# Attention and a two-layer MLP on one core: the last two token tiles as one 2×2 block problem

## The chip, the cores and the metric

The kernel runs on one core of one Trainium2 chip. The metric is the device time of one execution in microseconds (us), as the median of the runs shown. The core has a matmul engine (PE, with its weight loads listed apart as PEld), three elementwise engines (DVE, ACT and POOL) and a queue, SP, from which this kernel issues all its DMAs. Each engine works through its own queue in order; the engines wait for each other through semaphores.

## What is computed

Attention with a causal mask over 4 batches, 12 heads, 448 positions and 64 values per head, then a two-layer MLP over all 1792 tokens (768 to 2048 to 768):

```python
scores = scale * np.matmul(q, k.transpose(0, 1, 3, 2))
scores = np.where(mask, -1000000000.0, scores)
attn = np.exp(scores - np.max(scores, axis=-1, keepdims=True))
attn = attn / (np.sum(attn, axis=-1, keepdims=True) + 1e-09)
x = concat_heads(np.matmul(attn, v))            # 1792 x 768
h = x @ w_in                                    # 768 x 2048
g = np.where(h > 0.0, h, np.exp(np.minimum(h, 0.0)) - 1.0)
out = g @ w_out                                 # 2048 x 768
```

q, k and v are 32-bit floats, the two weight matrices 64-bit floats, which the kernel first turns into 32-bit ones on the chip.

## The kernel before

**Tiles.** The 448 positions are cut into four chunks of 112. A token tile is one chunk of all four batches: 4 x 112 = 448 columns. The text counts tiles from 1 to 4; the code's `g` counts from 0. Everything is kept transposed: features lie on the 128 partitions, tokens on the 448 columns. So layer 1 of a tile is 16 (`FT`) by 6 (`KT`) block products of 128x128 weights with 128x448 values, layer 2 is 6 (`ET`) by 16.

**A block product.** `three` (L580 to L585) computes one with three matmuls, to keep 32-bit precision: value and weight are each split into a rounded part and a rest (`xh`/`xl`, `gh`/`gl`; `whl` holds both parts of a weight piece), and high x high, high x low and low x high are summed in PSUM. The first 8 rows of layer 1 of tile 1 (`PLAIN`) use one plain 32-bit matmul instead (L599). A split costs one rounding copy (ACT, or DVE) and one subtraction (DVE, or POOL): L571, L572 and L574 for weight pieces, L316 and L318 for the attention's output, L611 and L612 for layer 1's.

**Order of the MLP.** `layers` (L633) goes through layer 1 row by row (`emit_h`, the ELU at L606 to L612 closes a row), then layer 2 (`emit_o`; L629 copies a finished row out of PSUM, L631 sends it). `weights` (L530) makes a weight piece: for tile 1 it loads 64-bit numbers, converts them (L547 to L558) and stores them as 32-bit in DRAM (L561); for tiles 2 to 4 it loads them back (L564). A piece is one row of layer 1 (768 columns) or, in layer 2, 768, 768 and 512 columns (`FG`).

**Attention.** `attention(g)` yields lumps of work: scores (L424, or L430 for tile 2), softmax (L269 on DVE, L273 on ACT), division by the sums (L500 to L506), transposes (L475), copies out of PSUM (L479, L480) and the product with the values (L454). Attention of tile 1 runs first, by itself. The loop at L646 to L660 then mixes each later tile's attention into the layers of the tile before it, in proportion: tile 2's beside tile 1's layers, tile 3's beside tile 2's, tile 4's beside tile 3's. Tile 4's layers have nothing beside them.

**Who orders the work.** Every operation is handed to `Plan.add` with its possible engines, a cost and a due time; `Plan.run` (L103) then lists the operations by due time against these costs and so fixes each engine's queue, and for operations with several `ways` also the engine. Buffers come from rings (`BUFS`, L226): five `w` tiles for raw weight pieces and eight `w6` tiles for split pieces are used in turn, so a load into `w` waits for all readers of the piece five places earlier.

## Time and profile before

| | us |
|---|---|
| median of 3 runs (lowest, highest) | 664.85 (663.88, 665.50) |
| profiled execution, its span from first to last instruction | 662.8 |
| busy: PE, PEld, DVE, ACT, POOL | 647.7, 550.8, 435.9, 414.5, 124.3 |
| granted TensorE clock, mean | 0.996 |
| DMA: bytes, share of 16 engines | 114.8 MB, 56.3% |

The profiled execution's own time is its span; the runs' times hold in addition what lies before the first and after the last instruction, 664.85 - 662.8 = 2.05 us at the median. Times in rows are us from the span's start, durations us or, where marked, ns. The busy time of an engine is the union of its records; neighbouring records overlap a little, so counts times mean durations come to more than the busy time.

### The profile page before, as it was taken

To read this page: it belongs to the slowest core of one execution; us is meant where nothing else is said; L and a number is where in the kernel's file an instruction comes from. 1 tells how busy PE (TensorE), PEld (TensorE's weight loads), DVE (VectorE), ACT (ScalarE), POOL (GpSimd) and SP (SyncE) were. 2 spreads that over 40 slices of the span, in tenths; PEclk is the share of its full clock that TensorE was granted. 3 is DMA by queue.
4 is the path that set the end of the run, shared out by engine and by line. 5 is a ranking of instruction groups with operands and counts; after the bars stand their busy time and mean duration, and the time that the engine had idled before them with its cause. 6 is when DMAs were issued, how large, how long until landed. Compare 5 with 4: busy or idle time off the path is not lost.

```text
span 662.8 us, 11710 instructions
## 1 busy us (share of the span) xinstructions
PE 647.7 (98%) x4176; PEld 550.8 (83%) x4176; DVE 435.9 (66%) x1032; ACT 414.5 (63%) x940; POOL 124.3 (19%) x104
## 2 busy tenths in 40 slices
PE   5899999999999999999999999999999999999997
PEld 4655588888878888888888888888888999999996
DVE  5866689786858897776562778687576447764310
ACT  6997999977549767675442987777565424443200
POOL 1353344343333212111000231102000100000000
PEclk9899999999999999999999999999999999999999
DMA  9999677788957464365564346364435543233210
GB/s 219 289 366 374 204 236 252 234 289 271 327 171 232 125 186 117 103 180 168 163 190 144 105 131 195 104 179 134 122 106 160 166 146 113 86 112 103 68 29 28
DMA packets 83577, 114.79 MB, mean 173 GB/s; under 512 B 39104, under 2 KB 59072, under 8 KB 83520
## 3 DMA queue, kind: packets, MB, share of 16 engines
q1 hardware_dynamic: 83520, 114.06, 56.3%
q8 instruction: 33, 0.54, 0.3%
q14 instruction: 24, 0.20, 0.1%
HBM read 95.94 MB, written 18.09 MB: 172 GB/s over the span
## 4 chain that ended last, share of the span: by engine, by line
PE 83%; ACT 10%; DVE 4%; issue 1%; POOL 1%; DMA 1%; SPq 0%; POOLq 0%; ACTq 0%; DVEq 0%
PE op L583 10%; PE op L585 10%; PE op L584 10%; PE hp L583 9%; PE hp L585 9%; PE hp L584 9%; PE av L454 6%; PE tr L475 6%; PE hp L599 6%; PE sc L424 5%; ACT a L273 3%; ACT w L551 2%; DVE whl L574 1%; ACT whl L571 1%; PE sc L430 1%
## 5 line engine op out<-in xcount | busy, mean ns | idle before, releaser
L574 DVE TENSOR_TENSOR whl<-w,whl 128x768 fp32r<-128x768 f32 (+1 forms) x118 | 114.3, 971 | 48.2 <-ACT whl L571 46.1
L583 PE MATMUL op<-gh,whl 128*128 128x448 f32 x384 | 143.4, 374 | 0.0
L585 PE MATMUL op<-gh,whl 128*128 128x448 f32 x384 | 141.1, 367 | 0.9 <-DVE whl L574 0.6
L584 PE MATMUL op<-gl,whl 128*128 128x448 f32 x384 | 140.4, 366 | 0.0
L583 PE MATMUL hp<-xh,whl 128*128 128x448 f32 x336 | 126.5, 376 | 0.3 <-ACT whl L571 0.3
L585 PE MATMUL hp<-xh,whl 128*128 128x448 f32 x336 | 122.9, 366 | 0.5 <-DVE whl L574 0.5
L584 PE MATMUL hp<-xl,whl 128*128 128x448 f32 x336 | 122.8, 366 | 0.0
L273 ACT ACTIVATE a<-a,nm 112x112 f32<-112x112 f32 (+3 forms) x192 | 96.9, 518 | 26.3 <-DVE nm L269 26.3
L269 DVE CUSTOM_DVE_ANT_0 a<-sc,mask 112x112 f32<-112x112 f32 (+3 forms) x192 | 75.1, 443 | 31.0 <-PE sc L424 20.8
L571 ACT ACTIVATE whl<-w 128x768 fp32r<-128x768 f32 (+1 forms) x69 | 53.9, 789 | 53.8 <-PE op L585 42.1
L583 PEld LDWEIGHTS op<-gh,whl 128*128 128x128 f32 x384 | 72.1, 188 | 9.8 <-issue 2.8
L585 PEld LDWEIGHTS op<-gh,whl 128*128 128x128 f32 x384 | 72.1, 188 | 9.2 <-DVE whl L574 3.2
L558 POOL TENSOR_TENSOR w<-w,w 128x768 int32<-128x768 int32 (+1 forms) x34 | 61.4, 1807 | 93.3 <-DVE w L552 42.8
L584 PEld LDWEIGHTS op<-gl,whl 128*128 128x128 f32 x384 | 72.2, 188 | 5.7
L583 PEld LDWEIGHTS hp<-xh,whl 128*128 128x128 f32 x336 | 63.1, 188 | 10.3 <-issue 4.7
L585 PEld LDWEIGHTS hp<-xh,whl 128*128 128x128 f32 x336 | 63.1, 188 | 6.1 <-DVE whl L574 0.9
L584 PEld LDWEIGHTS hp<-xl,whl 128*128 128x128 f32 x336 | 63.2, 188 | 4.8 <-issue 0.2
L608 DVE SCALAR_TENSOR_TENSOR hp<-m,hp 128x448 f32<-128x448 f32 x64 | 40.0, 625 | 30.4 <-ACT m L607 30.2
L606 ACT ACTIVATE m<-hp 128x448 f32<-128x448 f32 x64 | 34.7, 542 | 36.3 <-PE hp L585 34.8
L611 ACT ACTIVATE gh<-hp 128x448 fp32r<-128x448 f32 x64 | 34.3, 537 | 28.1 <-DVE hp L608 28.1
L612 DVE TENSOR_TENSOR gl<-hp,gh 128x448 fp32r<-128x448 f32 x64 | 39.7, 621 | 18.5 <-ACT gh L611 18.1
L454 PEld LDWEIGHTS av<-at,v 112*64 112x64 f32 x864 | 41.6, 137 | 12.1 <-issue 9.5
(57 smaller groups left out, 843.6 us busy)
## 6 DMA issues: line engine op xcount, KB each, us to landing
w<-w_i SPq DMA_DIRECT2D x48, 384.0 KB, 3.5
w<-w_o SPq DMA_DIRECT2D x36, 384.0 KB, 3.1
w<-in_w_in SPq DMA_DIRECT2D x16, 768.0 KB, 7.3
w<-in_w_out SPq DMA_DIRECT2D x12, 768.0 KB, 6.3
k<-in_qk SPq DMA_DIRECT2D x30, 224.0 KB, 4.1
w_i<-w SPq DMA_DIRECT2D x16, 384.0 KB, 5.2
q<-in_qk SPq DMA_DIRECT2D x24, 224.0 KB, 4.5
out_t<-ob SPq DMA_DIRECT2D x24, 224.0 KB, 3.0
```

What stands on the lines that cost most here:

```text
L269: plan.add(dve(n, lambda: nc.vector.tensor_tensor_reduce(out=a()[:, c], in0=sc()[:, c], in1=mask[:, S - n:], op0=ALU.add, op1=ALU.min, sca ...
L273: plan.add(act(n, lambda: nc.scalar.activation(a()[:, c], a()[:, c], AF.Exp, bias=nm()[:, x:x + 1], scale=-1.0, accum_out=su()[:, x:x + 1] ...
L454: nc.tensor.matmul(av()[half_of(half), chunk(o["b"])], o["v"]()[:, half, i], at()[:, chunk(x)], start=i == 0, stop=i == g,)
L475: nc.tensor.transpose(tr()[:, chunk(x)], o["a"][half]()[:, chunk(i)], ident)
L558: plan.add(pool(size, lambda: nc.gpsimd.tensor_tensor(out=wf().bitcast(I32), in0=wf().bitcast(I32), in1=low().bitcast(I32), op=ALU.add)), ...
L571: act(size, lambda: nc.scalar.activation(wh()[:, :n], w()[:, :n], AF.Copy)),
L574: sub = lambda eng: lambda: eng.tensor_tensor(out=wl()[:, :n], in0=w()[:, :n], in1=f32(wh()[:, :n]), op=ALU.subtract)
L583: nc.tensor.matmul(acc(), wh()[:, k], xh(), start=first, stop=False)
L584: nc.tensor.matmul(acc(), wh()[:, k], xl(), start=False, stop=False)
L585: nc.tensor.matmul(acc(), wl()[:, k], xh(), start=False, stop=last)
L599: pe(ONE, lambda: nc.tensor.matmul(hp(), w[0]()[:, k], x(), start=k == 0, stop=k == KT - 1), [*w, x], [hp], due)
L608: plan.add(dve(S, lambda: nc.vector.scalar_tensor_tensor(out=hp(), in0=m(), scalar=-1.0, in1=hp(), op0=ALU.add, op1=ALU.max)), [m], [hp])
```

## The change

Tiles 3 and 4 are no longer computed one after the other. Their layers become one problem of 2x2 blocks: the weights are cut in halves of rows and of inputs, the values in halves of features and in the two tiles. It is computed with seven block products of half size instead of eight, numbered 1, 2, 6, 7, 4, 5, 3 (`GROUPS`): layer 1 in `mixed_h`, layer 2 in `mixed_o`. The pieces of the method:

- **Values.** `halves` forms sums and differences of value blocks, four subtractions for each set of four blocks, before product 6; each product then splits its own 128x448 blocks into high and low (`split_row`).
- **Weights.** While tile 2's layers run, `mixed` forms the weight combinations with four additions per pair of pieces (on DVE or POOL, in place in the `w` tiles) and stores them in DRAM (`sin`, `sout`). To have both pieces of a pair at hand, tile 2 takes its rows in the order 0, 8, 1, 9 and so on, and its layer 2 in two accumulators side by side. The products read back pieces of 768 columns (`raw_piece`), 56 in all.
- **Results.** Products are combined as they finish: `results` keeps product 1 (`take`) and adds 6 and 7 to it (`plus`); products 2 and 3 go on in the PSUM bank of 1 and 5.
- **Layer 2 pieces** are 512 columns for all tiles, two runs of two blocks, so 24 pieces for 18.
- **Attention** of tiles 2, 3 and 4 is spread over the layers of tiles 1 and 2 alone (`SPREAD`, in units of the plan's matmul cost; the two tiles' layers are 246 such units). Tiles 3 and 4 have no attention beside them.
- **Buffers.** Tiles of 128x448 share one pool of places (`ROWS`), PSUM banks another; after the attention its places go to the new products (`lend`, `Heap`).

```diff
...
-    FG = ((0, 6), (6, 6), (12, 4))
+    HALF_F, HALF_K, HALF_E = FT // 2, KT // 2, ET // 2
+    NX = HALF_F // 2
...
-        xl = new("xl", [P, S], F32R)
+        if g >= 2:
+            x = xs[g, p] = new("x", [P, S], name="xs")
+            plan.add([
+                act(S, lambda: nc.scalar.activation(x(), av(), AF.Copy)),
+                dve(S, lambda: nc.vector.tensor_copy(x(), av())),
+            ], [av], [x])
+            return
...
-            f0, n = FG[key[2]]
-            src = w_out[key[1], :, f0:f0 + n]
+            two = slice(2 * key[2], 2 * key[2] + 2)
+            src, home = (
+                x[key[1]].rearrange("p (h f) c -> p h f c", h=2)[:, :, two] for x in (w_out, kout)
+            )
+            n = 4
...
-            k = kept[key] = Buf(None, lambda: dram.tile([P, n, P], F32, name=name))
+            k = kept[key] = Buf(None, lambda: home)
...
+    def mixed(layer, r, x, wa, wb):
+
+
+        h = HALF_K if layer == 1 else 2
+        n = h * P
+        blk = lambda w, half: lambda: w()[:, half * h:half * h + h]
+        a, b = (lambda half: blk(wa, half)), (lambda half: blk(wb, half))
+        add(b(1), b(0), b(1), n, ALU.add, [(wb, 0)], [(wb, 1)])
+        add(b(0), a(0), b(0), n, ALU.subtract, [(wa, 0)], [(wb, 0)])
+        add(a(0), b(1), a(0), n, ALU.subtract, [(wb, 1)], [(wa, 0)])
+        add(a(1), a(1), a(0), n, ALU.subtract, [(wa, 0)], [(wa, 1)])
+        k = skept[layer, r, x] = Buf(None, lambda: None)
+        home = sin[r] if layer == 1 else sout[x, :, :, :, r]
+        for i, w in enumerate((wa, wb)):
+            dma(2 * h * 64, 2 * P, lambda i=i, w=w: nc.sync.dma_start(
+                out=home[:, :, i], in_=w()[:, :2 * h].rearrange("p (h k) c -> p h (k c)", h=2)
+            ), [w], [(k, i)])
...
+            if g == 1 and f >= HALF_F:
+                plan.cap = due + LATER
+                mixed(1, f - HALF_F, None, wt[g, "i", f - HALF_F][3], wt[g, "i", f][3])
+                plan.cap = 1e9
...
-        x = f // FG[0][1]
-        if f == FG[x][0]:
+        x, i = f % HALF_F // 2, f // HALF_F * 2 + f % 2
+        if i == 0:
             weights(g, ("o", e, x))
-        if f == 0:
-            st["o"] = new("hp", [P, S], name="op")
-        op = st["o"]
+        first, last = x == i == 0, x == NX - 1 and i == 3
+        if i == 0 and g == 1 and e >= HALF_E:
+            plan.cap = due + LATER
+            mixed(2, e - HALF_E, x, wt[g, "o", e - HALF_E, x][3], wt[g, "o", e, x][3])
+            plan.cap = 1e9
...
+        fs = range(FT) if g == 0 else [f + h for f in range(HALF_F) for h in (0, HALF_F)]
+        for f in fs:
...
+        by_x = [(x, 2 * x + i + h) for x in range(NX) for h in (0, HALF_F) for i in range(2)]
+        for e in range(ET if g == 0 else HALF_E):
+            if g == 0:
+                todo = [(e, f) for _, f in by_x]
+            else:
+                todo = [(d, f) for x in range(NX) for d in (e, e + HALF_E) for y, f in by_x if y == x]
+            for d, f in todo:
+                yield THREE, lambda due, d=d, f=f: emit_o(g, d, f, due)
...
+    def halves(bs, i):
+
+        if i == 1:
+            return bs[0, 0]
+        if i == 2:
+            return bs[1, 0]
+        if i == 6:
+            t1, t2 = bs[0, 0], row("t2")
+            minus(t1, bs[0, 1], t1)
+            minus(t2, bs[1, 1], t1)
+            minus(bs[0, 1], bs[1, 1], bs[0, 1])
+            minus(bs[1, 0], bs[1, 0], t2)
+            return t2
+        return {7: bs[0, 1], 4: bs[1, 0], 5: bs[0, 0], 3: bs[1, 1]}[i]
...
+    def raw_piece(srcs, reads, dst):
+        w, t = new("ws", [P, KT, P], name="w"), new("w6s", [P, 2, KT, P], F32R, "whl")
+        dma(KT * 64, 2 * P, lambda: nc.sync.dma_start(out=dst(w()), in_=srcs), reads, [w])
+        hi_lo(lambda: t()[:, 0], lambda: t()[:, 1], w, KT * P, (t, 0), (t, 1), w)
+        ring("ws").done(w)
+        return t, (lambda k: t()[:, 0, k]), (lambda k: t()[:, 1, k])
...
+    GROUPS = ((1, 2), (6, 7, 4), (5, 3))
+    MIX = {6: (0, 0), 7: (0, 1), 3: (1, 0), 5: (1, 1)}
...
+        if i == 1:
+            keep["s", r] = row("s1")
+            take(keep["s", r], acc)
+        elif i == 6 or i == 7:
+            keep[i, r] = row("u")
+            plus(keep[i, r], acc, keep["s", r] if i == 6 else keep[6, r])
...
+        def item(g, i, r, k, due):
+            if k == 0:
+                if i not in (2, 3):
+                    st[r] = new("bank", [P, S], name="hp")
+                st["w", i, r] = weights_of(i, r)
+            acc, w, x = st[r], st["w", i, r], parts[i, k]
+            first = k == 0 and i not in (2, 3)
+            last = k == HALF_K - 1
+            pe(THREE, lambda: three(acc, w, k, x, first, last, i in (2, 3)), [w[0], *x], [acc], due)
+            if not last:
+                return
+            results(i, r, acc, keep)
+            if i == 2:
...
+            elif i == 4:
+                plus(acc, acc, keep[7, r])
+                G[1, 0, r] = keep["s", r]
+                elu(G[1, 0, r], acc)
+            elif i == 5:
+                G[1, 1, r] = keep[7, r]
+                plus(G[1, 1, r], acc, G[1, 1, r])
+                elu(G[1, 1, r], G[1, 1, r])
+            elif i == 3:
+                plus(acc, acc, keep[6, r])
+                G[0, 1, r] = keep[6, r]
+                elu(G[0, 1, r], acc)
+            if i not in (1, 5):
+                banks.done(acc)
+            if i in (2, 3) or i == 4 and r % 2 or i == 7:
+                ring("w6s").done(w[0])
...
+        for g in range(3):
+            for j in range(HALF_F // 2):
+                for i in GROUPS[g]:
+                    for r in (2 * j, 2 * j + 1):
+                        for k in range(HALF_K):
...
+            if e == f == 0:
+                st["w"] = weights_of(i, x)
+                st["x"] = []
+                for y in (2 * x, 2 * x + 1):
+                    b = halves({(a, c): G[a, c, y] for a in range(2) for c in range(2)}, i)
+                    st["x"].append(split_row(b))
+                    if i not in (1, 2):
+                        rows.done(b)
...
+            first = x == f == 0 and i not in (2, 3)
+            last = x == NX - 1 and f == 1
+            pe(THREE, lambda: three(acc, w, e * 2 + f, g, first, last, i in (2, 3)), [w[0], *g], [acc], due)
...
+        for i in (i for g in GROUPS for i in g):
+            for x in range(NX):
+                for e in range(HALF_E):
+                    for f in range(2):
+                        yield THREE, lambda due, a=(i, x, e, f): item(*a, due)
...
+    SPREAD = (0.0, 125.0, 185.0, 240.0)
...
+    ls = [(c, fn, g == 0) for g in range(2) for c, fn in layers(g)]
+    at = []
+    for g in range(1, NG):
+        items = list(attention(g))
+        all_c, done_c = sum(c for c, _ in items), 0.0
+        for c, fn in items:
+            at.append((SPREAD[g - 1] + (SPREAD[g] - SPREAD[g - 1]) * done_c / all_c, c, fn))
+            done_c += c
+    moved = 0.0
...
+            while at and at[0][0] <= moved:
+                _, ca, fa = at.pop(0)
+                fa(t)
+                t += ca * (SLOW if early else 1.0)
+                if not at:
+                    after_attention()
...
+    run([(c, fn, False) for c, fn in mixed_h()])
+    run([(c, fn, False) for c, fn in mixed_o()])
...
```

How this moves instructions is shown at three places. Names with a number are single buffers; `whl` is a split weight piece, `w` a raw one, `tr` and `at` attention weights before and after their copy out of PSUM, `sc` scores, `rr` reciprocal sums.

DVE in layer 2 of tile 2, beside attention; first before:

```order
L480 COPY at_3718<-tr_3674 112x336
L480 COPY at_3726<-tr_3676 112x336
L572 CAST whl_3788<-w_3533 128x768
L574 TENSOR_TENSOR whl_3788<-w_3533,whl_3788 128x768
L572 CAST whl_3791<-w_3613 128x768
L574 TENSOR_TENSOR whl_3791<-w_3613,whl_3791 128x768
L269 ISA a_3764,nm_3768<-sc_3760,mask_71 112x336
L269 ISA nm_3768 112x1
L269 ISA a_3765,nm_3768<-sc_3761,mask_71 112x336
L269 ISA nm_3768 112x1
```

and the change at the same place:

```order
L651 CAST whl_5304<-w_4970 128x512
L651 CAST whl_5306<-w_5128 128x512
L653 TENSOR_TENSOR whl_5306<-w_5128,whl_5306 128x512
L658 TENSOR_TENSOR w_5128<-w_5128 128x256
L544 COPY at_5318<-tr_5257 112x448
L544 COPY at_5325<-tr_5259 112x448
L336 RECIPROCAL rr_5215<-rr_5215 112x4
L653 TENSOR_TENSOR whl_5304<-w_4970,whl_5304 128x512
L658 TENSOR_TENSOR w_4970<-w_5128,w_4970 128x256
```

Between the splits (L653, formerly L574) there now stand the additions that mix weights (L658), and the low part of `whl_5304` stands behind two attention copies.

DVE near the end of layer 1 of the last tile; first before, where the ELU's last step (L608) and a split alternate:

```order
L572 CAST whl_6887<-w_6738 128x768
L574 TENSOR_TENSOR whl_6887<-w_6738,whl_6887 128x768
L608 SCALAR_TENSOR_TENSOR hp_6849<-m_6885,hp_6849 128x448
L612 TENSOR_TENSOR gl_6908<-hp_6849,gh_6903 128x448
L572 CAST whl_6919<-w_6770 128x768
L574 TENSOR_TENSOR whl_6919<-w_6770,whl_6919 128x768
```

and the change, near the end of layer 1 of tiles 3 and 4 (`hp` are PSUM accumulators, `u` and `s1` kept results; L777 is `plus`, L784 the ELU's last step, `hp_6494` and `hp_6514` hold product 5, on whose banks product 3 goes on):

```order
L777 TENSOR_TENSOR hp_6453<-hp_6453,u_6438 128x448
L777 TENSOR_TENSOR hp_6474<-hp_6474,u_6459 128x448
L784 SCALAR_TENSOR_TENSOR s1_6039<-m_6491,hp_6453 128x448
L653 TENSOR_TENSOR whl_6501<-w_6350,whl_6501 128x768
L777 TENSOR_TENSOR u_6145<-hp_6494,u_6145 128x448
L784 SCALAR_TENSOR_TENSOR s1_6050<-m_6507,hp_6474 128x448
L653 TENSOR_TENSOR pl_6536<-G_6011,ph_6518 128x448
L777 TENSOR_TENSOR u_6160<-hp_6514,u_6160 128x448
```

A row of layer 1 now ends with additions out of PSUM; `u_6145` and `u_6160` read banks that PE needs again.

SP in layer 2 of tile 2; before, in the same layer of tile 3, a load of weights (L564) stands among loads for attention:

```order
L564 DMA w_5246<-w32_o_0_0_1439 128x768
L564 DMA w_5250<-w32_o_0_1_1505 128x768
L386 DMA k_5252<-in_qk 128x448
L386 DMA k_5256<-in_qk 128x448
L387 DMA v_5269<-in_v 112x512
L387 DMA v_5276<-in_v 112x512
L564 DMA w_5310<-w32_o_0_2_1557 128x512
L564 DMA w_5332<-w32_o_1_0_1616 128x768
L386 DMA k_5361<-in_qk 128x448
```

and the change, where stores of mixed weights (L675) stand between the loads (L638) and each refill of a `w` tile follows such a store:

```order
L675 DMA sout_81<-w_4966 256x1x256
L675 DMA sout_81<-w_4898 256x1x256
L451 DMA v_5185<-in_v 112x512
L451 DMA v_5196<-in_v 112x512
L740 DMA out_t<-ob_5203 512x1x112
L638 DMA w_5229<-kout_79 128x2x256
L638 DMA w_5234<-kout_79 128x2x256
L451 DMA v_5314<-in_v 112x512
L451 DMA v_5323<-in_v 112x512
L675 DMA sout_81<-w_5128 256x1x256
L740 DMA out_t<-ob_5311 512x1x112
L675 DMA sout_81<-w_4970 256x1x256
```

## Rows read from the trace of the kernel before

**Rows 1.** The page, part 1: busy us, share of the span, instructions.

```profile
PE 647.7 (98%) x4176; PEld 550.8 (83%) x4176; DVE 435.9 (66%) x1032; ACT 414.5 (63%) x940; POOL 124.3 (19%) x104
```

**Rows 2.** Busy by stretch, layers of tiles 2, 3, 4: PE, PEld, DVE, ACT, POOL, clock, DMA.

```profile
198.30:364.80 166.50, 165.73 (x1159) 144.67 (x1159) 115.13 (x270) 104.96 (x250) 24.52 (x24) 1.00 0.54 160
364.80:541.10 176.30, 176.30 (x1294) 154.03 (x1291) 121.19 (x265) 116.45 (x251) 24.40 (x22) 1.00 0.46 140
541.10:658.50 117.40, 117.39 (x578) 108.10 (x576) 54.03 (x79) 35.08 (x61) 0.00 (x0) 1.00 0.28 83
```

**Rows 3.** Timeline of PE in layer 2 of tile 2, 28 starts apart.

```profile
299.68 0.36 PE L584 MATMUL op<-gl,whl 128*128 128x448 f32 x1
...
305.39 0.36 PE L585 MATMUL op<-gh,whl 128*128 128x448 f32 x1
```

**Rows 4.** Groups of DVE, POOL and ACT, shapes kept apart.

```profile
L574 DVE TENSOR_TENSOR whl<-w,whl 128x768 fp32r<-128x768 f32 x96 | 99.2, 1035 | 35.7 <-ACT whl L571 34.0
...
L612 DVE TENSOR_TENSOR gl<-hp,gh 128x448 fp32r<-128x448 f32 x64 | 39.7, 621 | 18.5 <-ACT gh L611 18.1
...
L574 DVE TENSOR_TENSOR whl<-w,whl 128x512 fp32r<-128x512 f32 x22 | 15.2, 690 | 12.5 <-ACT whl L571 12.1
L574 POOL TENSOR_TENSOR whl<-w,whl 128x768 fp32r<-128x768 f32 x8 | 14.8, 1854 | 73.2 <-ACT whl L571 33.9 <-PE sc L424 19.9 <-DVE whl L572 19.4
...
L629 ACT ACTIVATE ob<-op 128x448 f32<-128x448 f32 x24 | 13.0, 543 | 41.1 <-PE op L585 41.1
...
L368 POOL TENSOR_TENSOR khl<-k,khl 128x336 fp32r<-128x336 f32 x9 | 9.2, 1022 | 12.1 <-ACT khl L367 12.1
```

**Rows 5.** Busy by stretch, columns as above.

```profile
100.00:125.00 25.00, 25.00 (x160) 21.59 (x159) 21.73 (x51) 24.39 (x57) 10.14 (x7) 1.00 0.82 274
125.00:198.30 73.30, 72.31 (x440) 60.60 (x439) 54.13 (x113) 47.13 (x100) 27.20 (x16) 1.00 0.79 254
...
225.00:250.00 25.00, 25.00 (x182) 21.74 (x181) 22.37 (x50) 17.44 (x43) 4.93 (x5) 1.00 0.48 144
```

**Rows 6.** Timeline of the end: the last matmul and the last output's issue.

```profile
658.12 0.37 PE L585 MATMUL op<-gh,whl 128*128 128x448 f32 x1
...
659.14 0.53 SPq L631 DMA_DIRECT2D out_t<-ob  x1
```

**Rows 7.** DMA issues: KB each, median us to landing.

```profile
w<-w_o SPq DMA_DIRECT2D x18, 256.0 KB, 2.7
...
w_o<-w SPq DMA_DIRECT2D x6, 256.0 KB, 4.5
```

**Rows 8.** Waits of SP in front of weight loads.

```profile
SPq L564 <- DVE whl L574: 175.0, 71, 6.6
...
SPq L564 <- POOL whl L574: 50.3, 9, 10.0
```

**Rows 9.** Waits of PE: us in total, times, longest.

```profile
PE op L585 <- DVE whl L574: 0.6, 2, 0.3
```

**Rows 10.** Timeline of DVE and POOL, in layer 1 of tile 2.

```profile
228.33 1.16 POOL L368 TENSOR_TENSOR qhl<-q,qhl 128x448 fp32r<-128x448 f32 x1 [11.25 <-ACT qhl L367]
...
228.88 1.43 DVE L574 TENSOR_TENSOR whl<-w,whl 128x768 fp32r<-128x768 f32 x1
...
229.45 1.61 POOL L368 TENSOR_TENSOR khl<-k,khl 128x336 fp32r<-128x336 f32 x1
...
230.23 1.20 DVE L368 TENSOR_TENSOR khl<-k,khl 128x336 fp32r<-128x336 f32 x1
...
235.51 0.96 DVE L574 TENSOR_TENSOR whl<-w,whl 128x768 fp32r<-128x768 f32 x1
...
237.45 0.50 DVE L368 TENSOR_TENSOR khl<-k,khl 128x336 fp32r<-128x336 f32 x1
```

More of the change, by code (lines that the diff above doesn't have):

```diff
@@ L41, with __init__ @@
 class Ring:
-    def __init__(self, bufs, in_order=True):
-        self.bufs, self.in_order, self.bufs_of, self.order = bufs, in_order, [], []
+    def __init__(self, places, in_order=True, long=False):
+        self.long, self.in_order, self.places = long, in_order, places
+        self.free, self.bufs_of, self.order = [[] for _ in range(places)], [], []
     def new(self, make):
@@ L48, in new, with lend, after, __init__ @@
         self.bufs_of.append(b)
-        return b
+        if self.in_order:
+            b.before = self.free.pop(0)
+            for o in b.before:
+                o.after.append(b)
+            self.free.append([b])
+        return b
+    def lend(self, heap):
+        heap.free += self.free if self.in_order else [self.bufs_of[-2 * self.places:] for _ in self.free]
+        self.free = []
     def free_at(self, b, skip):
         n = len(self.order) + skip
-        if self.in_order and self.bufs_of[n] is not b:
-            return None
-        if n < self.bufs:
-            return 0.0
-        old = self.order[n - self.bufs]
-        return old.end if old.left == 0 else None
+        if not self.in_order:
+            if n < self.places:
+                return 0.0
+            old = self.order[n - self.places]
+            return old.end if old.left == 0 else None
+        if self.bufs_of[n] is not b:
+            return None
+        return self.after(b)
+    def after(self, b):
+        if any(o.left or not o.placed for o in b.before):
+            return None
+        return max([0.0] + [o.end for o in b.before])
+class Heap(Ring):
+    def __init__(self):
+        super().__init__(0)
+    def new(self, make):
+        b = super().new(make)
+        self.free.pop()
+        return b
+    def done(self, *bufs):
+        self.free += [[b] for b in bufs]
+    def free_at(self, b, skip):
+        return self.after(b)
 class Work:
@@ L109, in run @@
             dues = [s.due - lead for s in w.succs]
+            least = min(dues, default=1e9) - self.AHEAD
             for x in w.bufs:
-                if x.ring and x.n + x.ring.bufs < len(x.ring.bufs_of):
-                    dues.append(x.ring.bufs_of[x.n + x.ring.bufs].due - lead)
+                if x.ring and not x.ring.in_order:
+                    if x.n + x.ring.places < len(x.ring.bufs_of):
+                        dues.append(x.ring.bufs_of[x.n + x.ring.places].due - lead)
+                dues += [max(o.due - lead, least if x.ring.long else -1e9) for o in x.after]
             if w.due is None:
-                w.due = min(dues) if dues else 1e9
+                w.due = min([w.cap] + dues)
             for x in w.bufs:
@@ L320, in split_x @@
         xt[g, p] = xh, xl
-    first = [(new("gh", [P, S], name="q0"), new("gl", [P, S], name="k0")) for _ in range(NP)]
+    first = [(new("g", [P, S], name="q0"), new("g", [P, S], name="k0")) for _ in range(NP)]
     def first_pair(p, due):
@@ L574, in weights @@
-        sub = lambda eng: lambda: eng.tensor_tensor(
-            out=wl()[:, :n], in0=w()[:, :n], in1=f32(wh()[:, :n]), op=ALU.subtract
-        )
-        plan.add([dve(size, sub(nc.vector), port=True), pool(size, sub(nc.gpsimd))], [w, (t, 0)], [(t, 1)])
-        wt[(g, *key)] = t, wh, wl
-    def three(acc, w, k, x, first, last):
-        _, wh, wl = w
+            act(n, lambda: nc.scalar.activation(h(), x(), AF.Copy)),
+            dve(n, lambda: nc.vector.tensor_copy(h(), x()), 0.55e-3, 0.06, True),
+        ], [tx], [th])
@@ new lines, in layers, with row, split_row @@
+        for e in range(ET if g == 0 else HALF_E):
[5 more added lines that the diff above has]
+                yield THREE, lambda due, d=d, f=f: emit_o(g, d, f, due)
+    rows, banks = ring("row"), ring("bank")
+    def row(name, dtype=F32):
+        return new("row", [P, S], dtype, name)
+    def split_row(x):
+        h, l = row("ph", F32R), row("pl", F32R)
+        hi_lo(h, l, x, S, h, l, x)
+        return h, l
@@ new lines, in minus, with take, plus @@
+    def minus(out, x, y):
+        add(out, x, y, S, ALU.subtract, [b for b in (x, y) if b is not out], [out])
+    def take(out, acc):
+        plan.add([
+            act(S, lambda: nc.scalar.activation(out(), acc(), AF.Copy)),
+            dve(S, lambda: nc.vector.tensor_copy(out(), acc())),
+        ], [acc], [out])
+    def plus(out, acc, x):
+        plan.add(dve(S, lambda: nc.vector.tensor_tensor(out=out(), in0=acc(), in1=x(), op=ALU.add)),
+                 [b for b in (acc, x) if b is not out], [out])
```

227 lines of the change are left out of this document (183 added, 44 removed).

## The prediction

> **What bounds the kernel now.** I read the page's busy times first, then the busy time by stretch, then the timeline of PE, and the waits of PE and SP last. The page has PE busy for 647.7 of 662.8 us [rows 1], DVE for 435.9 and ACT for 414.5. That says PE, but a mean over the span could hide a stretch with another limit, so the next view is the busy time of each stage [rows 2]: tile 2's layers last 166.50 us with PE busy for 165.73, tile 3's 176.30 and tile 4's 117.40, both without a gap. The timeline shows what a busy PE does: 28 starts of matmuls in 5.71 us, 0.2039 each [rows 3]. Tile 4's stage, where nothing else stands on PE, gives the same: 117.40 us for 16x6x2 block products of three matmuls, 576 in all, 0.2038 each [rows 2]. So from 225 us on the end is a count of matmuls times 0.204 plus the attention's share of PE, and fewer matmuls end earlier as long as splits, weights and banks stay ahead of PE.
>
> **What goes.** For tiles 3 and 4, layer 1 had 2x96 block products and layer 2 again 2x96. Seven products of half size are 7x8x3 = 168 per layer for 192. That saves 48 block products, 144 matmuls, and the order of the change has 672 of each of the three kinds where there were 720. 144 x 0.2039 = **29.4 us** off PE. All of these stood in stages without a gap [rows 2], so all of it is on the path. The shares of attention on PE keep their number and only move.
>
> **What moves: the stage of tile 2.** It now holds its own layers with tile 3's attention (today's first row of [rows 2]) and tile 4's attention. The latter is the difference between the second and the third row: PE 176.30 - 117.40 = 58.9, DVE 121.19 - 54.03 = 67.2, ACT 116.45 - 35.08 = 81.4, POOL 24.4. Added to the first row: PE 166.5 + 58.9 = 225.4, DVE 182.3, ACT 186.3, POOL 48.9.
>
> On top come the additions that mix weights, four for each of 8 pairs of 384 columns and of 12 pairs of 256. The order gives DVE 17 and 34 of them, POOL 15 and 14. No row has these sizes. On DVE 512 columns take 0.690 and 448 0.621 [rows 4]; along that line 384 are an estimated 0.55 and 256 an estimated 0.41, 23.3 us together. On POOL 768 take 1.85 and 336 1.02 [rows 4], so an estimated 1.11 and 0.87, 28.8 us. The stage then has DVE at 205.6 us, ACT at 186.3 and POOL at 77.7 beside 225.4 of PE: 91%, 83% and 34%.
>
> Does PE stay full there? Between 225 and 250 us DVE was busy for 22.37 of 25 us and between 100 and 125 us ACT for 24.39, DVE for 21.73, and PE lost nothing in either; between 125 and 198 us PE lost 0.99 of 73.3, 1.35% [rows 5]. These are my bounds for the new waits of PE in this stage: 0 and 1.35%.
>
> **What comes: tiles 3 and 4.** PE: 1008 x 0.2039 = 205.5 us. DVE: twice tile 4's stage is 108.1. There are 77 splits of value blocks (21 in layer 1, 56 in layer 2) for 32 of `gl`; 11 go to POOL, so 34 more on DVE. There are 44 sums of value blocks, 33 on DVE, and 55 additions out of PSUM. That is 122 operations at 0.62 [rows 4], 75.6 us. Twelve fewer weight pieces (56 for 68, those of 512 columns) take off 8.3. In all 175.4, or 85% of the stage, below the 89% at which PE lost nothing. ACT: 70.2 and about 70 copies at 0.54 [rows 4], 108 us, half of the stage. The same bounds hold, 0 and 1.35%.
>
> Both stages are 431 us; the bounds make 0 to 5.8 us of waits. I take 2.8, the middle, since DVE is nearer to the full stretches but the queues are more entangled. 0.77 of it is in today's first row already [rows 2], so **+2.0**.
>
> **Edits that cost nothing.** Layer 2's pieces of 512 columns for 768: 1035 and 690 ns [rows 4] are the same per column, and the columns stay 12288. They cost something only if DMA becomes late: then the first tile's loads in shorter runs would be next. The end: the last result is now an addition on DVE (0.62) for a copy on ACT (0.54), 0.1 us; the last matmul starts at 658.12 and the output is issued at 659.14 [rows 6], and the three last outputs come some 1.2 us apart, each issue taking 0.53. The first 25 us don't change.
>
> **Sum.** 662.8 - 29.4 + 2.0 = 635.4 us of span; the profiled execution stands 2.05 us below the median of the runs, so **637.5 us** at the median. With no new waits 635.5, without today's either 634.
>
> **Rivals.**
> 1. *The bank comes late.* Product 3 goes on in the bank of product 5, after DVE has read it. After product 4's last matmul, PE has two rows of product 5, 18 x 0.204 = 3.67 us, before it wants `hp_6494` back. In that time the order has DVE do an addition, an ELU step and a split ahead of the reading addition: 0.62 + 0.62 + 1.04 + 0.62 = 2.9. That leaves 0.8, less the hops. Eight rows of layer 1 have this, and eight the same with product 1, 2 and the copy between. Before, a row had its own bank and nothing waited. If DVE stands one split and one ELU step further behind, 1.66 less 0.8 makes 0.9 at each of the 16 places, and 14 us come back: 651.5. Against it: DVE has idle time in that stage, and product 1's copy has only ACT in front.
> 2. *The `w` tiles come late.* 40 pieces in 225.4 us is one per 5.6, so with five places one may be held for 28 us. Now a place is held for the load (2.7), the split (0.63 estimated and 0.69), the partner's piece (5.6), four additions (up to 3.5) and the store (4.5) [rows 4, 7]: 17.6, so 10.4 us cover it. But SP waits for splits in front of weight loads today, 175.0 us in 71 waits for DVE and up to 10.0 at once for POOL [rows 8], and the queue is in order: a store that waits for a mixing addition holds up the loads behind it. If the weights of each of the 20 pairs came 0.7 us late, 14 us: 651.5. PE's waits for splits are 0.6 us in two waits today [rows 9].
> 3. *DVE and POOL in each other's way: slower than before.* At 228.33 and 229.45 POOL ran subtractions of 1.16 and 1.61; beside them a DVE subtraction took 1.43 that takes 0.96 undisturbed, and one 1.20 that takes 0.50 [rows 10]. So 1.17 of 2.77 us of POOL, 42%, were added to DVE. If every microsecond of POOL in tile 2's stage did that, DVE would need 205.6 + 77.7 = 283.3 us for 225.4, 57.9 over: 693. It decides from 225.4 - 205.6 + 29.4 = 49.2 of the 77.7 us, or 63%, on. Against it: from 100 to 125 us DVE and POOL together were busy for 31.9 of 25 us [rows 5], and the means I used contain today's share already. At 42% of all 77.7, DVE is 12.8 over: 648, near the top of my range. The Trainium skill ("SBUF — State Buffer", section "Who interferes with whom") states it as a rule: a DVE instruction with two SBUF inputs and a POOL instruction that reads SBUF shut each other out for the whole instruction; all mixing additions are of that kind, and by that rule alone this rival's 693 would be the sum. The trace agrees in kind at 228 us, but not in extent.
> 4. *The change doesn't do what it says.* The order excludes that by the count above. A slower matmul would do the same; at 0.204 both with attention beside it and alone [rows 2, 3], nothing speaks for one.
>
> **Chances.** The forecast, 634 to 643, 0.65; rival 1, 643 to 652, 0.12; rival 2, 643 to 658, 0.12; rival 3, from 665 on, 0.05; fewer waits than today, below 634, 0.06. The range of 634 to 649 leaves out the last two and the upper part of rival 2, some 0.18. A measurement of this kernel tells 0.3% (2 us) from no change: faster 0.93, same 0.02 (the far end of rival 2), slower 0.05.
>
> **What would show it.** Right: 2016 matmuls in the split form, still 0.204 apart in the last 200 us, no attention beside them; tile 2's last product some 59 us later than today's 364.8 and PE idle between the two by 2 to 3 us; tiles 3 and 4 in about 206. Rival 1 would show as waits of PE for DVE or ACT at the first matmul of products 2 and 3; rival 2 as waits for weight splits in tile 2's layer 2, with SP waiting for L675's additions; rival 3 as DVE at 98% or more there, subtractions far over 1.04, PE waiting for softmax and attention copies. The forecast is wrong if PE is idle for over 8 us after 200 us, or the matmuls' step is not 0.204.

## The result and the profile after

Beside four runs of before at 664.63 us (663.88 to 665.5), the changed kernel took **644.74 us** at the median of four (643.83 to 646.43): 0.9702 of before, 95% interval 0.9685 to 0.9719. That is 19.9 us faster, inside the range of 634 to 649, but 7.2 us above the forecast of 637.5.

The profiled execution took 645.02 us with a span of 643.2. Its first part, to hold against [rows 1], is

```profile
PE 620.4 (96%) x4032; PEld 523.9 (81%) x4032; DVE 517.0 (80%) x1192; ACT 441.4 (69%) x1007; POOL 192.4 (30%) x166
```

PE is busy for 27.2 us less than before where 29.4 were forecast, and idle for 22.8 us where it was 15.1. The busy times of stretches (the columns are those of [rows 5]) show where:

```profile
36.00:80.00 44.00, 44.00 (x195) 23.57 (x195) 31.18 (x81) 38.95 (x87) 17.76 (x14) 1.00 0.82 289
80.00:100.00 20.00, 18.22 (x122) 14.56 (x120) 18.12 (x42) 16.33 (x40) 9.17 (x6) 1.00 0.69 221
100.00:125.00 25.00, 23.77 (x119) 20.51 (x119) 21.90 (x51) 21.07 (x46) 9.21 (x8) 0.86 0.68 217
125.00:207.00 82.00, 80.42 (x512) 67.97 (x511) 62.77 (x151) 57.37 (x136) 29.41 (x23) 1.00 0.85 266
207.00:300.00 93.00, 92.51 (x748) 78.84 (x747) 85.66 (x226) 81.78 (x214) 45.07 (x39) 1.00 0.69 217
300.00:431.00 131.00, 129.84 (x1102) 110.03 (x1101) 113.32 (x272) 94.84 (x219) 40.53 (x41) 1.00 0.67 208
431.00:643.20 212.20, 206.33 (x1007) 188.46 (x1006) 159.29 (x244) 102.53 (x176) 29.85 (x21) 1.00 0.36 106
```

The stages that the prediction was about are nearly full: PE loses 0.49 and 1.16 us in tile 2's (207 to 431 us). The loss stands ahead of them, in tile 1's, which had lost nothing between 100 and 125 us before [rows 5]. Now PE is idle there and its granted clock falls to 0.86. The timeline of PE at that place (start, duration, and in brackets the idle time and its releaser):

```profile
97.21 1.01 PE L494 MATMUL sc<-k,q 64*112 64x224 f32 x8
101.23 0.74 PE L682 MATMUL hp<-xh,whl 128*128 128x448 f32 x1 [3.01 <-ACT whl L650]
...
102.76 0.58 PE L682 MATMUL hp<-xh,whl 128*128 128x448 f32 x1
103.14 0.58 PE L683 MATMUL hp<-xl,whl 128*128 128x448 f32 x1
...
107.24 0.57 PE L682 MATMUL hp<-xh,whl 128*128 128x448 f32 x1
107.61 0.40 PE L683 MATMUL hp<-xl,whl 128*128 128x448 f32 x1
107.85 0.36 PE L684 MATMUL hp<-xh,whl 128*128 128x448 f32 x1
```

PE stands still for 3.01 us, and after it the matmuls start 0.373 apart (102.76 to 107.61) where they start 0.204 apart otherwise: the lower of the clock's two levels, with 0.50 granted from 102 to 106 us. From 101.23 to 107.85, 17 matmuls take 6.62 us where 17 x 0.204 is 3.47: another 3.15 us. The first and the last matmul of tile 1's layers, first before, then in the change, are

```profile
35.41 1.40 PE L599 MATMUL hp<-xf,w 128*128 128x448 f32 x3
...
198.36 0.36 PE L585 MATMUL op<-gh,whl 128*128 128x448 f32 x1
```
```profile
34.96 1.40 PE L703 MATMUL hp<-xf,w 128*128 128x448 f32 x3
...
204.89 0.36 PE L684 MATMUL op<-gh,whl 128*128 128x448 f32 x1
```

The stage takes 169.93 us for 162.95, 6.98 more. Some 1.1 of these are work brought forward: 12 score matmuls of tile 3, which before come after this stage. The other 5.9 are lost.

What made the split late? DVE, POOL and ACT ahead of it:

```profile
98.03 1.20 DVE L335 TENSOR_SCALAR rr<-su 112x4 f32<-112x4 f32 x1
```
```profile
95.53 3.66 POOL L631 TENSOR_TENSOR w<-w,w 128x768 int32<-128x768 int32 x2 [3.25 <-DVE w L625]
```
```profile
99.53 0.48 ACT L567 ACTIVATE a<-a,rr 112x224 f32<-112x224 f32 x1 [1.11 <-DVE rr L336]
99.92 0.52 ACT L710 ACTIVATE m<-hp 128x448 f32<-128x448 f32 x1
100.35 0.83 ACT L650 ACTIVATE whl<-w 128x768 fp32r<-128x768 f32 x1
```

A DVE instruction on four columns, 0.16 us elsewhere, takes 1.20 and ends at 99.23, when a row of two POOL additions ends (99.19); it began during the second of them. ACT's queue stands for it, with the split behind. The order of the program says why POOL has two in a row here: piece 13's addition stands ahead of piece 12's, whose raw tile `w64_719` gives up its place to piece 11's split. Before, they stood in sequence.

```
L631 TENSOR_TENSOR w_1069<-w_1069,w64_680 128x768
L631 TENSOR_TENSOR w_1113<-w_1113,w64_815 128x768
L631 TENSOR_TENSOR w_1106<-w_1106,w64_719 128x768
```

From 430.62 us (first matmul of tiles 3 and 4) to 639.04 (end of the last) it is 208.4 us for 205.5 forecast. The waits of PE by releaser (us in total, times, longest) show rival 1 in small, in the second line:

```profile
PE hp L682 <- ACT whl L650: 3.0, 1, 3.0
PE hp L682 <- DVE u L777: 1.7, 3, 1.0
```

### The profile page after: what moved, and what is told of

Read it like the earlier page. It is cut to its first block, busy times and chain, and to the rows that moved or that the text cites. A ratio compares the mean times of both kernels' runs of the same rounds, so it can differ in the third digit from the quotient of the medians.

```text
span 643.2 us, 11841 instructions
## 1 busy us (share of the span) xinstructions
PE 620.4 (96%) x4032; PEld 523.9 (81%) x4032; DVE 517.0 (80%) x1192; ACT 441.4 (69%) x1007; POOL 192.4 (30%) x166
## 5 line engine op out<-in xcount | busy, mean ns | idle before, releaser
L653 DVE TENSOR_TENSOR whl<-w,whl 128x768 fp32r<-128x768 f32 (+1 forms) x114 | 108.1, 952 | 17.8 <-ACT whl L650 16.3
L631 POOL TENSOR_TENSOR w<-w,w 128x512 int32<-128x512 int32 (+1 forms) x40 | 62.7, 1569 | 98.3 <-DVE w L625 70.8
L682 PE MATMUL op<-gh,whl 128*128 128x448 f32 x192 | 73.3, 382 | 1.5 <-ACT whl L650 1.4
L684 PE MATMUL op<-gh,whl 128*128 128x448 f32 x192 | 70.9, 369 | 1.3 <-DVE whl L653 1.2
L683 PE MATMUL op<-gl,whl 128*128 128x448 f32 x192 | 70.1, 365 | 0.0
L682 PE MATMUL hp<-ph,whl 128*128 128x448 f32 x168 | 61.9, 369 | 1.7 <-DVE u L777 1.7
L682 PE MATMUL op<-ph,whl 128*128 128x448 f32 x168 | 61.5, 366 | 0.0
L684 PE MATMUL op<-ph,whl 128*128 128x448 f32 x168 | 61.5, 366 | 0.0
L683 PE MATMUL op<-pl,whl 128*128 128x448 f32 x168 | 61.5, 366 | 0.0
L683 PE MATMUL hp<-pl,whl 128*128 128x448 f32 x168 | 61.5, 366 | 0.0
L684 PE MATMUL hp<-ph,whl 128*128 128x448 f32 x168 | 61.4, 366 | 0.0
L682 PE MATMUL hp<-xh,whl 128*128 128x448 f32 x144 | 57.1, 396 | 3.0 <-ACT whl L650 3.0
L684 PE MATMUL hp<-xh,whl 128*128 128x448 f32 x144 | 53.9, 374 | 0.2 <-DVE whl L653 0.2
L683 PE MATMUL hp<-xl,whl 128*128 128x448 f32 x144 | 53.6, 372 | 0.0
L518 PE MATMUL av<-at,v 112*64 112x112 f32 x864 | 49.4, 263 | 0.0
L658 POOL TENSOR_TENSOR w<-w 128x384 f32<-128x384 f32 (+1 forms) x29 | 27.1, 933 | 63.2 <-DVE w L658 29.4
```

The source lines that it names most:

```text
L518: nc.tensor.matmul(av()[half_of(half), chunk(o["b"])], o["v"]()[:, half, i], at()[:, chunk(x)], start=i == 0, stop=i == g,)
L631: plan.add(pool(size, lambda: nc.gpsimd.tensor_tensor(out=wf().bitcast(I32), in0=wf().bitcast(I32), in1=low().bitcast(I32), op=ALU.add)), ...
L653: sub = lambda eng: lambda: eng.tensor_tensor(out=l(), in0=x(), in1=f32(h()), op=ALU.subtract)
L658: two = lambda eng: lambda: eng.tensor_tensor(out=out(), in0=x(), in1=y(), op=op)
L682: nc.tensor.matmul(acc(), wh(k), xh(), start=first, stop=False, skip_group_check=more)
L683: nc.tensor.matmul(acc(), wh(k), xl(), start=False, stop=False, skip_group_check=more)
```

## The experiments

Theory at first: the missing 7 us are the one stop at 98 us, made by the inverted order of two additions. Rivals: the load of DVE and ACT; the size of layer 2's pieces; the mixing additions; the bank of product 5. Four runs each unless another number is given; before stood at 664.4 to 664.7 us beside them.

**e1, the additions in order.** Each piece's last addition of the conversion comes after that of the piece before:

```diff
-            plan.add(pool(size, lambda: nc.gpsimd.tensor_tensor(
+            st["add"] = plan.add(pool(size, lambda: nc.gpsimd.tensor_tensor(
...
-            )), [(r, 0)], [w])
+            )), [(r, 0)], [w], after=st.get("add"))
```

> The changed kernel, with one more dependence: in tile 1's stage the last addition of each weight piece's conversion (L631, POOL) may not stand ahead of that of the piece before it. In the changed kernel the order on POOL has piece 13 (`w_1113<-w64_815`) ahead of piece 12 (`w_1106<-w64_719`); the split `whl` of piece 11 is written into the place of piece 12's raw tile, so it waits for both. Theory: this one inversion is where the missing gain went. PE waited 3.01 us at 98.2 us for ACT's `whl` and then ran at a granted clock of 0.58 to 0.73 until 107.6 us, 16 matmuls at 0.373 for 0.204, 2.6 us. Without it both go: 644.7 - 5.3 = 639.4 us, range 638.5 to 641, with no wait of PE over 1.2 us between 40 and 190 us. Rival, load: DVE and ACT were busy for 21.9 and 21.1 of the 25 us around the wait, so it returns at another piece: 643 to 646, with PE's waits between 80 and 140 us still 2.5 us or more.

Measured: 644.64 us (644.16 to 648.61), no gain. Yet what was to happen in tile 1's stage did: the stop at 98 us and the half clock are gone (0.8 us of waits are left there), and with the same matmuls in it the stage takes 166.38 us for 169.93, 3.55 less:

```profile
34.00 1.40 PE L703 MATMUL hp<-xf,w 128*128 128x448 f32 x3
...
200.38 0.37 PE L684 MATMUL op<-gh,whl 128*128 128x448 f32 x1
```

At its end PE is 4.5 us ahead, as in this execution the layers also began 1.0 us earlier. That beginning lies between 34.0 and 36.1 us in the profiles of this record; it sets a limit to what a single profile can say. But by 344.58 us (344.68 in the changed kernel) both have the same result out. 3.9 of the 4.5 us go in one stop and the half clock behind it (0.375 apart from 229.34 on), 25 us into tile 2's stage:

```profile
224.91 0.41 PE L488 MATMUL sc<-khl,qhl 64*112 64x336 f32 x1
227.52 1.18 PE L488 MATMUL sc<-khl,qhl 64*112 64x336 f32 x11 [2.21 <-DVE xs L375]
...
229.34 0.57 PE L682 MATMUL hp<-xh,whl 128*128 128x448 f32 x1
229.72 0.57 PE L683 MATMUL hp<-xl,whl 128*128 128x448 f32 x1
```

POOL's timeline ahead of that stop, and DVE's scalings L564 beside it (shortest, median and longest of the two, in ns):

```profile
222.90 0.67 POOL L570 TENSOR_SCALAR a<-a,rr 112x336 f32<-112x336 f32 x1 [1.25 <-DVE rr L336]
223.54 1.01 POOL L658 TENSOR_TENSOR w<-w 128x384 f32<-128x384 f32 x1
224.52 1.75 POOL L432 TENSOR_TENSOR khl<-k,khl 128x336 fp32r<-128x336 f32 x2
```
```profile
L564 DVE TENSOR_SCALAR a<-a,rr x2: 395/1890/3386, 222.8 to 223.1; 112x336 f32<-112x336 f32 x2
```

One scaling took 3.39 us for 0.40: from 223.1 to 226.45, while four POOL instructions ran back to back until 226.27. So the first theory fell as far as the total goes, and a wider one takes its place: **lock-out**. A DVE instruction waits out a whole row of POOL instructions; where DVE's queue is full, PE stops. That such a wait alone costs nothing the changed kernel itself shows: at 375.74 us a scaling took 2.93 us for 0.44 beside three POOL instructions, and PE had no gap between 372 and 390 us. The rival is DVE's load: it was busy for 9.93 of the 10 us from 218 to 228.

**e2, the kernel before with pieces of 512.**

```diff
-    FG = ((0, 6), (6, 6), (12, 4))
+    FG = ((0, 4), (4, 4), (8, 4), (12, 4))
```

> The kernel before, with layer 2's weights in four pieces of 512 columns for three of 768, 768 and 512, and nothing else. Its order has the additions of pieces 12 and 13 in sequence. Theory (the inversion, not the size): six more pieces are hidden work, and the time stays within 1.5 us of before, 663.5 to 666; PE's waits between 40 and 207 us rise by less than 1.5 us. Rival, size: the pieces themselves cost the missing 7 us, by their fixed shares of seven instructions and two transfers each: 668 to 672, with new waits of PE for `whl` from 100 us on.

Measured in ten runs: 666.35 us, 1.0027 of before (1.0018 to 1.0037), 1.2 to 2.5 us more. PE's waits between 40 and 207 us rise from 1.4 to 3.1, and tile 1's stage takes 164.87 us for 162.95. Both expectations missed: the pieces themselves cost about 2 us, not nothing and not 7.

**e3, no mixing additions.**

```diff
-        add(b(1), b(0), b(1), n, ALU.add, [(wb, 0)], [(wb, 1)])
-        add(b(0), a(0), b(0), n, ALU.subtract, [(wa, 0)], [(wb, 0)])
-        add(a(0), b(1), a(0), n, ALU.subtract, [(wb, 1)], [(wa, 0)])
-        add(a(1), a(1), a(0), n, ALU.subtract, [(wa, 0)], [(wa, 1)])
```

> The changed kernel without the 80 additions that mix weights in tile 2's stage; the stores stay, so tiles 3 and 4 read unmixed weights (this part of the computation is left out). Theory: PE stays full in tile 2's stage without them as with them, where its waits are 2 us in all; they cost at most 1 us: 643.5 to 645.5. Rival (the port between DVE and POOL, and the stores that wait for the additions): they cost 3 us or more of the missing gain: below 642.

Measured: 642.23 us (641.98 to 643.1), 2.5 less. In the profiled execution 2.0 us are there at the end of tile 1's stage (last matmul at 202.90 for 204.89), which has no mixing additions: 0.6 since its layers began earlier, 1.4 by a shorter stretch of half clock. From there to the first matmul of tiles 3 and 4 it is 224.3 us for 225.7, so the mixing additions cost some 1.4 us. The time fell between the two expectations; whether the other three executions had the shorter half clock too, no trace shows.

**e4, four rows of layer 1 at a time** (the test for the last step changes with it).

```diff
-            for j in range(HALF_F // 2):
+            for j in range(HALF_F // 4):
                 for i in GROUPS[g]:
-                    for r in (2 * j, 2 * j + 1):
+                    for r in range(4 * j, 4 * j + 4):
```

> The changed kernel with layer 1's products of tiles 3 and 4 done for four rows of the result at a time, not two, so that between product 5's last read and product 3 in the same bank PE has four rows of work, not two. Theory: the waits of PE for DVE's reading addition (1.71 us in three waits at 523 to 534 us) go, and the time falls by 1 to 1.7 us: 643 to 643.8. Rival: the hand-over is set by DVE's queue, not by the distance, and the waits stay within 0.5 us of 1.7: 644.3 to 645.2. A third way, slower: four rows hold four split weight tiles of eight, the next ones come late, and PE waits for them: over 646.

Measured: 642.24 us (640.99 to 643.43), 2.5 less, which is more than any of the expectations had. PE has no wait for L777 any more; the stop at 98 us is still there. From the first to the last matmul of tiles 3 and 4 it is 205.4 us (430.74 to 636.17) for 208.1. That is rival 1, 1.7 us of waits and a little more.

**e5, splits of queries and keys on DVE alone**: e1, and in `parts`

```diff
-        plan.add([dve(n, sub(nc.vector), port=True), pool(n, sub(nc.gpsimd))], [x, (t, 0)], [(t, 1)])
+        plan.add([dve(n, sub(nc.vector), port=True)], [x, (t, 0)], [(t, 1)])
```

> The kernel of e1, with the splits of queries and keys for the attention of tiles 3 and 4 (L432) on DVE alone; in e1 27 of them stand on POOL in tile 2's stage, 29.1 us. In e1 PE lost 2.21 us at 225.3 us to a DVE copy that stood behind two scalings (L564), and those took 3.69 us for 0.8, beside POOL's unbroken row of three lines (L570, L658, L432) from 222.90 to 226.27. Theory, lock-out: not DVE's load but such rows of POOL instructions stop PE. Without L432 on POOL the row is broken, the stall at 225 us and the half clock behind it (1.7 us) go: 644.6 - 3.9 = 640.7 us, range 639.5 to 642. Rival, load: the 27 splits put some 15.4 us on DVE (0.50 to 0.62 each), which is busy for 9.9 of 10 us there; the stall stays or grows: 644.5 to 650.

Measured: 647.38 us (644.97 to 648.62), inside the load theory's range. The row at 222.9 us is broken, but PE stops for 2.08 us at 227 us all the same, now for ACT's `m`: three scalings L564 took 4.23 us from 217.01 on, beside a new row of L653 and three L658 on POOL from 217.02 to 222.14. Here each scaling waited out one POOL instruction, not the row (2.05, 1.17 and 1.17 us). This run can't tell lock-out and load apart, since it did both.

**e6, e1 and e4 together.**

> e1 and e4 together. The two edits lie in different stages (tile 1's, and layer 1 of tiles 3 and 4). If what e1 gains in tile 1's stage is lost again in tile 2's whatever comes later: e1's 644.6 less e4's 2.5 is 642.1, range 641 to 643, with the wait of some 2.2 us at 225 us there again. If that second wait was chance of one execution and not of the order: below 640.

Measured: 642.75 us (642.26 to 645.61), with a stop of 2.19 us near 227 us, behind the same scaling (3.38 us) and the same row of four. So the stop belongs to the order, not to one execution. The clock did not fall behind it this time, and the time is no better than e4's.

**e7, e4 and e5 together.**

> e4's and e5's edits together. By the lock-out theory the three gains add: 640.7 - 2.5 = 638.2 us, range 637 to 639.5. By load: 642 or more.

Measured: 643.09 us (642.06 to 646.54), again in the load theory's range, with the stop of e5, 2.09 us. As in e5.

**e8, one product of layer 2 less.**

```diff
-            pe(THREE, lambda: three(acc, w, e * 2 + f, g, first, last, i in (2, 3)), [w[0], *g], [acc], due)
+            if i != 2:
+                pe(THREE, lambda: three(acc, w, e * 2 + f, g, first, last, i in (2, 3)), [w[0], *g], [acc], due)
```

> The changed kernel without the matmuls of product 2 in layer 2 of tiles 3 and 4; its weight pieces, splits and results stay (a seventh of that layer's product is left out). It prices a product as the sum of the prediction did: 72 matmuls x 0.204 = 14.7 us, so 644.7 - 14.7 = 630.0, range 629 to 631, and the same for the two products that the change saves. Rival: DVE, busy for 76% of that stage, has the work of the product's stretch still to do, and part of the 14.7 us is not gained: 632 or more.

Measured: 631.08 us (630.51 to 632.46): 13.7 us for 72 matmuls, 93% of the price. The waits for L777 grow from 1.7 to 2.2 us, half of what is missing.

**e9, e6 without the mixing additions.**

> e6 without the 80 additions that mix weights (that part is left out, as in e3). In e6 the 5.3 us gained in tile 1's stage are lost again in tile 2's, at 225 to 235 us, where DVE is busy for 9.9 of 10 us. Theory: DVE and POOL together set the pace of the first third of tile 2's stage, so what is gained ahead of it is only kept if work there goes. Without the mixing additions the wait of some 2.2 us and the half clock behind it (1.7 us) go, and the gains add: 642.75 - 3.9 - 1 (what e3 gained in tile 2's stage) = 637.9 us, range 636.5 to 639. Rival: the second stall has another cause (a load, a place); it stays, and e3's 2.5 us alone come off: 640.2, range 639.5 to 642.

Measured: 639.15 us (637.92 to 640.1), just over the theory's range and below its rival's. The stop near 227 us is gone, with no half clock. But the gains of e3 and e4 alone, 2.5 us each, would make 639.7: of e1's gain in tile 1's stage little reaches the time even here, and e3's own gain was in part one of that stage.

**e10, attention spread wider**: e6, and

```diff
-    SPREAD = (0.0, 125.0, 185.0, 240.0)
+    SPREAD = (0.0, 125.0, 187.0, 241.0)
```

> e6 with attention of tile 3 spread until 187 in place of 185 and that of tile 4 until 241 in place of 240 of the planner's units, which takes 3% of the attention out of the first part of tile 2's stage. By the same theory the stall at 225 us shrinks to under 1 us and the half clock goes with it: 639 us, range 638 to 641. Rival: 3% is too little, 642 to 643.5, with a wait of 2 us there. A third way: the attention of tile 4 ends late, and PE waits over 1 us between 395 and 432 us: over 643.

Measured: 642.91 us (642.25 to 643.51), where the theory had 638 to 641. The stop near 227 us is gone, and another stands at 337 us, 2.08 us, with a granted clock of 0.57 behind it. Again a DVE instruction, L653, took 4.46 us for 0.68, beside a row of four:

```profile
334.52 0.64 POOL L570 TENSOR_SCALAR a<-a,rr 112x448 f32<-112x448 f32 x1 [4.16 <-ACT khl L431]
335.13 2.25 POOL L432 TENSOR_TENSOR khl<-k,khl 128x448 fp32r<-128x448 f32 x2
337.34 1.26 POOL L653 TENSOR_TENSOR whl<-w,whl 128x512 fp32r<-128x512 f32 x1
```
```profile
L653 DVE TENSOR_TENSOR whl<-w,whl x2: 679/2569/4459, 334.7 to 339.1; 128x512 fp32r<-128x512 f32 x2
...
  PE op L684: 2.1, 1
```

**e11, the mixing additions on DVE alone as well**: e7, and in `add` the way by `pool` for rows of S elements only

```diff
-        plan.add([dve(n, two(nc.vector), port=True), pool(n, two(nc.gpsimd))], reads, writes)
+        plan.add([dve(n, two(nc.vector), port=True)] + [pool(n, two(nc.gpsimd))] * (n == S), reads, writes)
```

> e7 with the additions that mix weights on DVE alone as well, so that in tile 2's stage POOL has only the subtractions of weight splits and some scalings, and no rows of three or more. Lock-out theory: what stops PE are the rows of POOL instructions that a DVE scaling waits out (3.39 us for one in e1 at 223.1 us); without them 638 to 640 us. Load theory: 30 additions go to DVE at 0.41 to 0.55 each, 14 us, and DVE, at 88.5 of 93 us between 207 and 300 us in e7, has no room: more waits there, 644 us or more.

Measured: 641.42 us (639.95 to 643.1), 0.9646 of before (0.9618 to 0.9674). The time lies between the two expectations (638 to 640, 644 or more); the profile speaks for the first. e6 first, then e11, from 207 to 300 us:

```profile
207.00:300.00 93.00, 90.24 (x733) 76.31 (x732) 88.36 (x215) 78.88 (x206) 43.10 (x40) 1.00 0.64 201
```
```profile
207.00:300.00 93.00, 92.37 (x761) 78.16 (x760) 89.59 (x241) 84.20 (x216) 20.44 (x16) 1.00 0.65 206
...
431.00:639.00 208.00, 204.64 (x1002) 187.76 (x1001) 158.61 (x247) 104.41 (x180) 31.26 (x20) 1.00 0.37 108
```

DVE is busier, 89.59 for 88.36, and PE loses 0.63 us for 2.76. More load on DVE did not stop PE, so POOL's rows are the better reading of the stop near 227 us. It rests on one order against another: e10 moved the stop by a change of order alone. Not all of the gain is kept: there are waits of 1.5 us at 395 us and of 1.4 at 440, the clock staying at 1.00, and the time is not told apart from e4's.

**e12, POOL idle in tiles 3 and 4**: e11, no way by `pool` in `add`, and none in `hi_lo` as `raw_piece` and `split_row` call it. Five runs.

```diff
-        plan.add([dve(n, sub(nc.vector), port=True), pool(n, sub(nc.gpsimd))], [tx, th], [tl])
+        plan.add([dve(n, sub(nc.vector), port=True)] + [pool(n, sub(nc.gpsimd))] * (not alone), [tx, th], [tl])
```

> e11 with the splits and subtractions of tiles 3 and 4 (weight pieces and value blocks) on DVE alone, so that POOL does nothing there. Lock-out theory: PE's wait of 1.39 us at 440 us goes with POOL's instructions, and nothing comes in its place, as DVE (158.6 of 208 us) has room for the some 15 us more, of which some 8 us are given back as DVE waits out no POOL instruction: 641.4 - 1.4 = 640.0 us, range 639 to 641.5. Load theory: DVE is later at each hand-over of splits and banks, and PE's waits there grow: 642 us or more.

Measured: 642.45 us (641.26 to 643.18), not told apart from e11, and in the load theory's range, though PE's waits at the hand-overs did not grow. The wait at 440 us is gone, and the profiled execution's span is 639.4 us, but the median did not follow. What the run shows is a price. In e11 POOL had 20 instructions in that stage, 31.3 us; on DVE they take 18 x 0.617 + 2 x 0.954 = 13.0 us. With POOL idle, DVE's own instructions get shorter, e11 first (count, busy time, mean ns of one):

```profile
L784 DVE SCALAR_TENSOR_TENSOR u<-m,u 128x448 f32<-128x448 f32 x8 | 6.3, 787 | 0.0
L658 DVE TENSOR_TENSOR G<-u,G 128x448 f32<-128x448 f32 x5 | 5.6, 1112 | 0.1
```
```profile
L784 DVE SCALAR_TENSOR_TENSOR u<-m,u 128x448 f32<-128x448 f32 x8 | 4.8, 616 | 0.2 <-ACT m L783 0.2
L658 DVE TENSOR_TENSOR G<-u,G 128x448 f32<-128x448 f32 x8 | 4.8, 616 | 0.0
```

Over the seven groups with the largest differences, count times difference of the means is 7.7 us, as the expectation had it. So in this stage POOL took 13.0 us off DVE and gave 7.7 back as waiting.

## Why the prediction was right, and where it was not

**What goes** held: e8 gives 13.7 us for a product where the sum had 14.7, and the two that the change saves are 27 to 29 us.

**What moves** held. Tile 2's stage, from its first layer matmul at 206.29 to the first of the next at 430.62, is 224.3 us; with the 24 score matmuls brought forward (2.2 us) 226.5, where 225.4 and some wait were forecast. DVE was forecast at 205.6 us, ACT at 186.3 and POOL at 77.7; from 207 to 431 us they have 199.0, 176.6 and 85.6.

**What comes** was 2.9 us short: 208.4 for 205.5, of which 1.7 is the bank of rival 1, at three of its sixteen places, with DVE busy for less than forecast (159.3 for 175.4). e4 shows it by taking it away. Both stages together are 4.0 us over their 431, of which the allowance for new waits covers 2.0.

**"Edits that cost nothing" is the step that failed.** It costed layer 2's pieces of 512 columns at nothing, since their instructions cost the same per column, and looked no further into tile 1's stage than its first 25 us. That start is indeed unchanged; the stage then loses 5.9 us. That is most of the 7.8 us by which the span missed its 635.4. By the runs: pieces of 512 alone cost about 2 us (e2); the order of two conversions, inverted by the planner, costs 3.55 us in that stage (e1; 3.6 to 3.9 in the profiles of e5 to e7 and e9 to e12, which have that edit too). Together they are nearly the whole 5.9. In the planner's rules a piece of 4 blocks is due sooner than one of 6; that this earlier date is what inverted the order was read from the code and not tried on its own. It can't be the date alone, as e2 has the same pieces and those two additions in sequence.

**The range held for another reason than the one it was widened for.** The prediction put 0.65 on 634 to 643; 644.74 lies where it had rivals 1 and 2. Rival 1 is there with 1.7 us. Of rival 2's sign, waits for weight splits in tile 2's stage, there are 1.4 us in three waits. Most of the excess is the loss in tile 1's stage, which no rival names; that it was no larger than the room left for them is luck.

**Rival 3 had the right mechanism at the wrong scale.** It made a rate of it: 42% of POOL's time added to DVE, from one place. e12 gives 7.7 of 31.3 us, 25%, in the last stage. And where PE stopped, it was not for the sum over tile 2's stage, in which DVE still had room (199.0 of 224 us); it was for a row: up to four POOL instructions back to back, behind which one DVE instruction stands for as long as 4.5 us, and PE behind it. The Trainium skill ("SBUF — State Buffer", section "Who interferes with whom") has the second of two such instructions, one on each engine, blocked until the first has finished; in e1 and e10 the block lasted for a row of four, not for one.

**That one stop hides the next** was no part of the prediction, and is what e1 shows: PE was 4.5 us ahead at the end of tile 1's stage and lost it at the next stop. The likely reason is that DVE caught up while PE stood at 98 us, and that without this pause the next row of POOL met a full queue; no run tries it by itself. e9 and e11 have no such stop, the one by less work, the other by shorter rows, but little of the 3.55 us is seen in their times. In e11's profile tile 2's stage, from the last matmul of tile 1's layers to the first of the next stage, takes 1.4 us more than in the changed kernel (227.2 for 225.7; e1 230.1), and the last stage 1.6 us more than in e4 (207.1 for 205.4), with the wait at 440 us. Whether these could go as well stays open.

The fastest kernel here that does the whole computation is e11, 641.42 us, and its interval lies below the changed kernel's; e4, e6, e7, e10 and e12 are not told apart from it.

## What to carry to other kernels

An edit that is hidden work by its sum can still move a planner's order far from the place it is for: compare the whole order, first where two engines have no room. Count against work that POOL takes off DVE that more than half of the relief (7.7 of 13.0 us here) can come back as waiting, and look at how many such instructions stand in a row beside a DVE instruction that something waits for. A stop of PE that lets the clock fall cost one and a half times to twice its length here, and taking one stop away is only worth what the next one leaves.

## What the hardware showed that was not expected

A DVE scaling of 0.40 us took 3.39 us beside four POOL instructions back to back (e1; 3.38 in e6), a subtraction of 0.68 took 4.46 (e10), and one on four columns 1.20 for 0.16 beside the rest of one POOL addition (98.03 us): each ended as POOL's work ended, or later by less than its own undisturbed time. In the rows of e1, e6 and e10 each POOL instruction starts before the one ahead has ended; in the row of e5 they stand 0.08 us apart, and a scaling got through between each two. What decides which of the two happens was not tried.

Stops of PE of 2.21 (e1), 2.08 (e10) and 3.01 us were followed by the lower clock, 1.7 to 3.15 us of loss each. After stops of 2.08 (e5), 2.19 (e6) and 2.09 us (e7), and of 1.35 and 1.5 us, the granted clock stayed at 1.00. So of two stops of nearly the same length one was followed by the lower clock and another was not.
